# Read weights turned by VectorE blocks and on-chip transfers instead of TensorE, and one store per 128 state rows

## The chip, the core and the metric

The kernel runs on one core of a Trainium2 chip. The core has a matrix engine (PE in the profile, with PEld for its weight loads), three elementwise engines (DVE, the vector engine; ACT, the scalar engine; POOL), a sync engine SP, and 16 DMA engines. DMAs here are issued by the sequencers of SP and ACT; each sequencer issues in program order and stops at the first DMA whose wait isn't met. The metric is the device time of one execution in microseconds. Measured time before: 678.72 us, the median of three runs (678.38 to 679.03).

## What is computed

```python
# x: [8 batches, 8 heads, 512 tokens, 64], state: [8, 8, 32 states, 64]
scores  = scale * x @ state^T              # [B, H, 512, 32]
a       = softmax over the 32 states
xread   = a @ state                        # tokens read the states
scores2 = scale * state @ x^T              # [B, H, 32, 512]
a2      = softmax over the 512 tokens
sread   = a2 @ x                           # states read the tokens
rows    = concat(xread, sread) over tokens # 8 * (512 + 32) = 4352 rows of 8 * 64 = 512
out     = relu(rows @ w_in)**2 @ w_out     # w_in 512 x 2048, w_out 2048 x 512
```

All of it is float32. The two large products are computed as three passes over high and low parts of the operands (`hi*hi + lo*hi + hi*lo`).

## The kernel before

**Per batch, the tokens.** Head products are packed: a tile of 128 rows is 4 heads (`HG`) times 32 states (`N`), and there are two such groups (`NG`). `scores` (L198) multiplies the states with the transposed tokens `xt_raw` into the PSUM tile `pst`. From it the softmax over states is made with the states turned onto the free axis: VectorE's 32x32 block transpose `turn1` (L245) into the tile `q1`, maximum, subtraction, exponential, sum, division, and the block transpose back, `turn2` (L278), into the tile `at`; then `at` is split into the parts `a_hi` (ScalarE) and `a_lo` (GpSimd for batches 2 to 7). The state is multiplied into `w_in` beforehand (`z_piece`, L131: tiles `pz`, `z_hi`, `z_lo`), so that the up product of the MLP is `ph = z^T a` (L364), six matmuls of 512 columns per block of 128 hidden units. ScalarE applies the relu (`r`), VectorE squares in place, ScalarE rounds to `g_hi`, VectorE subtracts to `g_lo`, and twelve matmuls (L407) add the block into four PSUM tiles `po`. Such a step of 6 + 12 matmuls is repeated 16 times per batch, and the down product of a block is issued two blocks after its up product.

**Per batch, the states.** `keep` (L217) copies `pst` to the tile `e`, and `exps2` (L220) makes the exponentials of the softmax over tokens in it, with the row sums in `s2`. To multiply them with the tokens, the tokens have to lie on the partitions. `turn` (L308) does that with eight 128x128 TensorE transposes into the PSUM tile `pt` and one ScalarE copy to the tile `e_t` (L316). `read` (L318) then multiplies `e_t` with the tokens `xn_raw` in 32 small matmuls, one per group, head and block of 128 tokens (L325, tile `pr`), VectorE scales by the row sums (`rd`, L330), and GpSimd puts the result into the row tile `sr`. After the last batch the 256 state rows go through the same MLP in a stage of their own (`states`, L826), which ends the program: its two output tiles of 128 rows are copied from PSUM and stored (L858).

**What sets the order.** Batches 0 and 1 up to their last up product are ordered by an explicit list scheduler (`Plan`); everything after is emitted in slots, two per step of 18 matmuls. A queue of attention steps (`reads`) is worked off over the slots so that each batch's is done in time; the table `lags` says how many slots a step must lie behind another (L579 to L581). The states' read of batch b - 2 is queued ahead of the scores of batch b. A scheduler behind the source then moves instructions by a model of its own, and the order on each engine is fixed when the program is built. All these PSUM tiles (`pst`, later `pz`, `pt`, `pr`) share one buffer, tag `px`. The SBUF tile `e_t` shares its buffer with `at` (tag `at`, one buffer), so `e_t` of a batch can only be written when both parts have been made from the next batch's `at`.

Of the kernel before, what the change touches and what calls it, by code (L numbers as in the profile page):

```python
# [9 lines left out]
F32 = mybir.dt.float32  # L10
# [8 lines left out]
def memory_attention_then_relu2_ffn(  # L19
# [21 lines left out]
    nc = tc.nc  # L41
    P = 128
    B, S, C = xn.shape
    D = stP.shape[1] // 2
    H = C // D
    N = stP.shape[2] // (H // 2)
    DM, DF = w_out.shape[1] // 2, w_out.shape[0]
    R = S + N
    NG = H * N // P
    HG = H // NG  # L50
    NCC = DM // P
    NFC = DF // P
    NT = S // P
    ZC = 4
    GB = P // N
# [10 lines left out]
    sb = ctx.enter_context(tc.tile_pool(name="sb", bufs=2))  # L66
    ps_o = ctx.enter_context(tc.tile_pool(name="ps_o", bufs=4, space=bass.MemoryType.PSUM))
    ps_h = ctx.enter_context(tc.tile_pool(name="ps_h", bufs=2, space=bass.MemoryType.PSUM))
    ps_x = ctx.enter_context(tc.tile_pool(name="ps_x", bufs=1, space=bass.MemoryType.PSUM))
# [5 lines left out]
    ident = const.tile([P, P], F32, name="ident")  # L75
# [15 lines left out]
    def split(*args):  # L91
        for step in parts_of(*args):
            step()
# [76 lines left out]
    def attention(b):  # L170
        NJ = S // 32
        pair, my = [], {}
# [133 lines left out]
            return turn1, soft1, soft1b, soft1c  # L306

        def turn():  # L308
            pt = ps_x.tile([P, NG, NT, P], F32, name="pt", tag="px")
            for g in range(NG):  # L310
                for t in range(NT):
                    nc.tensor.transpose(  # L312
                        out=pt[:, g, t, :], in_=my["e2"][:, g, t * P:(t + 1) * P], identity=ident
                    )
            my["e"] = sb.tile([P, NG, NT, P], F32, name="e_t", tag="at", bufs=1)
            nc.scalar.copy(out=my["e"], in_=pt)  # L316

        def read():  # L318
            pr = ps_x.tile([P, NG, S], F32, name="pr", tag="px")
            with tc.high_priority(offset=HURRY):  # L320
                for g in range(NG):
                    for t in range(NT):
                        for j in range(HG):
                            h = g * HG + j
                            nc.tensor.matmul(  # L325
                                pr[j * N:(j + 1) * N, g, :D], lhsT=my["e"][:, g, t, j * N:(j + 1) * N],
                                rhs=my["n"][:, t, h * D:(h + 1) * D], start=t == 0, stop=t == NT - 1,
                            )
            rd = sb.tile([P, NG, D], F32, name="rd", bufs=1)
            nc.vector.tensor_mul(  # L330
                out=rd, in0=pr[:, :, :D], in1=my["s2"].rearrange("p (g o) -> p g o", o=1)
                .broadcast_to([P, NG, D])
            )
            at = (b % GB) * N
            for j in range(HG):
                nc.gpsimd.tensor_copy(  # L336
                    out=sr[b // GB][at:at + N, j * NG * D:(j + 1) * NG * D],
                    in_=rd[j * N:(j + 1) * N].rearrange("p g d -> p (g d)"),
                )

        steps = dict(
            pad=pad, load_t=load_t, scores=scores, keep=keep, exps2=exps2, load_n=load_n, turn=turn,
            read=read,
        )
        return pair, steps, [soft(gs) if b < 2 else grouped(*soft(gs)) for gs in halves]
# [87 lines left out]
    def move(t, dst, po):  # L433
        if t % 2:
            nc.scalar.copy(out=dst, in_=po)
        else:
            nc.vector.tensor_copy(out=dst, in_=po)
# [35 lines left out]
    begins, ends, at = {}, {}, {}  # L473
# [102 lines left out]
    lags = {}  # L576
    for b in range(B):
        _, w, softs = attentions[b]
        lags[w["exps2"]] = [(w["scores"], 1)]  # L579
        lags[w["turn"]] = [(w["exps2"], 1)]  # L580
        lags[w["read"]] = [(w["turn"], 1)]  # L581
        if b > 1:
            lags[softs[0][2]] = [(softs[0][1], 1)]

# [14 lines left out]
    for n, (b, fcs) in enumerate(parts):  # L599
        i = fcs[0]  # L600
# [225 lines left out]
    def states():  # L826
        NS = B * N
        x2 = []

        def turn2(i):  # L830
            def run():
                if not x2:
                    x2.extend(
                        sb.tile([P, NCC, NS], F32R, name=n, tag=t, bufs=2)
                        for n, t in (("x2_hi", "a_hi"), ("x2_lo", "a_lo"))
                    )
                own = slice(i * P, (i + 1) * P)
                pt = ps_x.tile([P, NCC, P], F32, name="pt2", tag="px")
                for cc in range(NCC):
                    nc.tensor.transpose(  # L840
                        out=pt[:, cc, :], in_=sr[i][:, cc * P:(cc + 1) * P], identity=ident
                    )
                split(x2[0][:, :, own], x2[1][:, :, own], pt, nc.vector)
            return run

        def first(fc):
            while reads.done < len(reads.steps):
                reads.next()
            w_hi = sb.tile([P, NCC, P], F32R, name="wi_hi", tag="z_hi", bufs=2)
            w_lo = sb.tile([P, NCC, P], F32R, name="wi_lo", tag="z_lo", bufs=2)  # L850
            split(w_hi, w_lo, wi[:, :, fc * P:(fc + 1) * P], nc.vector)
            return [
                (w[:, cc, :], v[:, cc, :])
                for w, v in ((w_hi, x2[0]), (w_lo, x2[0]), (w_hi, x2[1]))
                for cc in range(NCC)
            ]

        def rows(t, po):  # L858
            tile_ = sb.tile([P, DM], F32, name="os_", tag="raw", bufs=RAW)
            move(t, tile_, po)  # L860
            for i in range(GB):
                at = (t * GB + i) * R + S
                queue = nc.scalar if i % 2 else nc.sync
                queue.dma_start(out=out[at:at + N, :], in_=tile_[i * N:(i + 1) * N, :])

        reads.add([turn2(i) for i in range(NGB)], 2 * ends[B - 1] - 2, 2 * ends[B - 1] - 8)
        return dict(width=NS, fcs=range(NFC), first=first, rows=rows)

    mlp([batch(*p) for p in parts] + [states()], begin, aux)
# [34 lines left out]
```

## Time and profile before

| | |
|---|---|
| median of three runs | 678.72 us |
| the profiled execution | 678.34 us, of which 676.2 us lie between its first and last instruction (the span) |
| PE busy | 646.4 us, 96% of the span |
| DVE, ACT, POOL busy | 368.0, 288.9, 24.3 us |
| DMA | 43.59 MB in 15803 packets |
| TensorE transposes of the read weights | 64 |
| ScalarE copies of the transposed weights | 8 |
| stores of state rows | 8, of 64 KB each |

The page gives the busy time of each engine, its busy share in 40 slices of the span, the chain of work that ended last, and groups of instructions by source line. The trace behind it answers for single lines, for tiles (by name), and for stretches of time. In a timeline row the numbers are the start and the duration in us, then engine, line, operation, output and input tiles, shape and count; in brackets stands how long the engine had been idle and who ended that. Several equal instructions in a row are merged: the duration is then from the first start to the last end.

### The profile page before, as it was taken

To read this page: it belongs to the slowest core of one execution; us is meant where nothing else is said; L and a number is where in the kernel's file an instruction comes from. 1 tells how busy PE (TensorE), PEld (TensorE's weight loads), DVE (VectorE), ACT (ScalarE), POOL (GpSimd) and SP (SyncE) were. 2 spreads that over 40 slices of the span, in tenths; PEclk is the share of its full clock that TensorE was granted. 3 is DMA by queue.
4 is the path that set the end of the run, shared out by engine and by line. 5 is a ranking of instruction groups with operands and counts; after the bars stand their busy time and mean duration, and the time that the engine had idled before them with its cause. 6 is when DMAs were issued, how large, how long until landed. Compare 5 with 4: busy or idle time off the path is not lost.

```text
span 676.2 us, 9543 instructions
## 1 busy us (share of the span) xinstructions
PE 646.4 (96%) x3864; PEld 492.8 (73%) x3864; DVE 368.0 (54%) x522; ACT 288.9 (43%) x468; POOL 24.3 (4%) x44
## 2 busy tenths in 40 slices
PE   1788999999999999999999999999999999999996
PEld 0465876777777777777777877777778767888995
DVE  4899789346557336533483347433563254333553
ACT  3567665344435335333442335323353233333442
POOL 0000000000101000100010000100010000000000
PEclk9999999999999999999999999999999999999999
DMA  8534560013040005000310005000301001000101
GB/s 318 187 131 181 182 230 31 1 67 126 34 153 5 1 0 189 4 1 1 127 65 0 1 1 188 0 1 1 126 1 63 1 1 62 1 0 1 63 1 32
DMA packets 15803, 43.59 MB, mean 64 GB/s; under 512 B 1296, under 2 KB 3344, under 8 KB 13840
## 3 DMA queue, kind: packets, MB, share of 16 engines
q1 hardware_dynamic: 15568, 42.73, 17.3%
q8 instruction: 30, 0.49, 0.3%
q10 hardware_dynamic: 192, 0.26, 0.2%
q14 instruction: 13, 0.11, 0.1%
HBM read 34.08 MB, written 8.91 MB: 64 GB/s over the span
## 4 chain that ended last, share of the span: by engine, by line
PE 89%; DVE 7%; issue 1%; ACT 1%; DMA 1%; SPq 0%; DVEq 0%; ACTq 0%
PE po L407 53%; PE ph L364 28%; PE pz L154 4%; PE pr L325 1%; PE pst L204 1%; PE pt L312 1%; DVE wof L114 1%; DMA xt_raw<-xT 1%; DVE wo_lo L87 1%; DVE z_lo L87 1%; DVE wi L114 1%; DVE wi L120 1%; DVE wi L108 0%; DVE g_lo L87 0%; DVE a_lo L87 0%
## 5 line engine op out<-in xcount | busy, mean ns | idle before, releaser
L407 PE MATMUL po<-wo_hi,g_hi 128*128 128x512 f32 x544 | 215.4, 396 | 0.1
L407 PE MATMUL po<-wo_lo,g_hi 128*128 128x512 f32 x544 | 213.5, 392 | 0.8 <-DVE wo_lo L87 0.8
L369 ACT ACTIVATE r<-ph 128x512 f32<-128x512 f32 (+1 forms) x144 | 82.9, 576 | 174.4 <-PE ph L364 174.0
L407 PE MATMUL po<-wo_hi,g_lo 128*128 128x512 f32 x544 | 154.3, 394 | 0.0
L377 DVE TENSOR_TENSOR ph<-ph,r 128x512 f32<-128x512 f32 (+1 forms) x128 | 84.9, 663 | 126.0 <-ACT r L369 125.6
L87 DVE TENSOR_TENSOR g_lo<-ph,g_hi 128x512 fp32r<-128x512 f32 (+1 forms) x144 | 94.7, 658 | 73.9 <-ACT g_hi L84 44.5
L84 ACT CAST g_hi<-ph 128x512 fp32r<-128x512 f32 (+1 forms) x144 | 81.0, 563 | 110.3 <-DVE ph L377 79.3
L407 PEld LDWEIGHTS po<-wo_hi,g_hi 128*128 128x128 f32 x544 | 102.2, 188 | 29.6 <-ACT g_hi L84 4.4
L407 PEld LDWEIGHTS po<-wo_lo,g_hi 128*128 128x128 f32 x544 | 102.2, 188 | 27.9 <-issue 5.0
L407 PEld LDWEIGHTS po<-wo_hi,g_lo 128*128 128x128 f32 x544 | 100.3, 188 | 28.0 <-issue 7.1
L364 PE MATMUL ph<-a_hi,z_lo 128*128 128x512 f32 x256 | 82.8, 402 | 3.2 <-DVE z_lo L87 3.2
L364 PE MATMUL ph<-a_hi,z_hi 128*128 128x512 f32 x256 | 82.4, 403 | 3.0 <-ACT a_hi L84 2.0
L364 PE MATMUL ph<-a_lo,z_hi 128*128 128x512 f32 x256 | 80.2, 395 | 0.0
L87 DVE TENSOR_TENSOR z_lo<-pz,z_hi 128x1024 fp32r<-128x1024 f32 (+2 forms) x37 | 39.7, 1078 | 52.4 <-ACT z_hi L84 52.3
L364 PEld LDWEIGHTS ph<-a_hi,z_lo 128*128 128x128 f32 x256 | 47.9, 190 | 23.0 <-issue 8.4
L364 PEld LDWEIGHTS ph<-a_hi,z_hi 128*128 128x128 f32 x256 | 47.8, 190 | 18.3 <-ACT a_hi L84 2.7
L84 ACT CAST z_hi<-pz 128x1024 fp32r<-128x1024 f32 (+2 forms) x37 | 32.9, 899 | 55.9 <-PE ph L364 34.6
L364 PEld LDWEIGHTS ph<-a_lo,z_hi 128*128 128x128 f32 x256 | 48.7, 190 | 10.8
L154 PE MATMUL pz<-wi,sp_raw 64*32 64x512 f32 (+2 forms) x560 | 36.4, 579 | 10.7 <-DVE wi L120 8.6
L154 PEld LDWEIGHTS pz<-wi,sp_raw 64*32 64x32 f32 x560 | 6.5, 107 | 25.1 <-DVE wi L120 10.2
L336 POOL COPY sr<-rd 32x128 f32<-32x128 f32 x32 | 9.2, 289 | 384.5 <-DVE rd L330 383.4
L246 DVE STREAM_TRANSPOSE q<-pst 128x1024 f32<-128x1024 f32 (+1 forms) x9 | 10.1, 1126 | 19.7 <-ACT e L218 11.1
(61 smaller groups left out, 381.6 us busy)
## 6 DMA issues: line engine op xcount, KB each, us to landing
xt_raw<-xT SPq DMA_DIRECT2D x8, 1024.0 KB, 5.5
wo_raw<-w_out SPq DMA_DIRECT2D x8, 1024.0 KB, 5.7
xn_raw<-xn SPq DMA_DIRECT2D x8, 1024.0 KB, 5.5
out<-sum SPq DMA_DIRECT2D x32, 256.0 KB, 3.5
wi_raw<-w_in SPq DMA_DIRECT2D x7, 1024.0 KB, 4.8
wi_raw<-w_in SPq DMA_DIRECT2D x2, 512.0 KB, 7.1
sp_raw<-stP SPq DMA_DIRECT2D x8, 64.0 KB, 1.8
out<-os__5348 SPq DMA_DIRECT2D x2, 64.0 KB, 1.7
```

Of the source, the lines that this page charges most:

```text
L84: nc.scalar.copy(out=hi, in_=src)
L87: eng_lo.tensor_sub(out=lo, in0=src, in1=hi.bitcast(F32))
L114: nc.vector.scalar_tensor_tensor(out=bits, in0=high, scalar=-0x80000000, in1=bits, op0=ALU.bitwise_and, op1=ALU.bitwise_or,)
L120: mark[:] = [nc.vector.scalar_tensor_tensor(out=bits, in0=low, scalar=29, in1=bits, op0=ALU.logical_shift_right, op1=ALU.bitwise_or,)]
L154: nc.tensor.matmul(pz[g][j * N:(j + 1) * N], lhsT=state[b][rows, j, :], rhs=wi[rows, j, cols], start=True, stop=True,)
L204: nc.tensor.matmul(pst[j * N:(j + 1) * N, g, :], lhsT=state[b][rows, j, :], rhs=my["t"][rows, j, :], start=True, stop=True,)
L246: nc.vector.transpose(out=my["q1"][:, gs].rearrange("p g j n -> p (g j n)"), in_=my["pst"][:, gs].rearrange("p g s -> p (g s)"),)
L336: nc.gpsimd.tensor_copy(out=sr[b // GB][at:at + N, j * NG * D:(j + 1) * NG * D], in_=rd[j * N:(j + 1) * N].rearrange("p g d -> p (g d)"),)
L364: nc.tensor.matmul(ph, lhsT=w, rhs=v, start=m == 0, stop=m == len(todo) - 1)
L369: nc.scalar.activation(r, my[0], AF.Relu)
L377: nc.vector.tensor_mul(out=ph, in0=ph, in1=r)
L407: nc.tensor.matmul(po[t], lhsT=g, rhs=w, start=i == 0 and j == 0, stop=i == last and j == 2)
```

## The change

`turn` no longer uses TensorE, PSUM or ScalarE. VectorE transposes the whole of `e` in 32x32 blocks into a new tile `eq`, which shares the buffer of `q1` (tag `q1`, one buffer). A 32x32 block transpose leaves each block where it was, so sixteen SBUF-to-SBUF transfers per batch, all on SP's queue, move the blocks to their places: the transfer for head `j` and token block `i` takes 32 partitions of `eq` with 2 x 4 pieces of 32 numbers (128 bytes) each, to 32 partitions of `e_t`. `e_t` has the same contents, addressed with the head as a dimension. `read` must now lie at least four slots behind `turn`, not one. At the end of the program each 128-row tile of state rows is stored by one transfer with an output pattern of 4 x 32 x 512, one on SP's queue and one on ACT's, instead of four transfers of 32 x 512, two on each.

```diff
         def turn():
-            pt = ps_x.tile([P, NG, NT, P], F32, name="pt", tag="px")
-            for g in range(NG):
-                for t in range(NT):
-                    nc.tensor.transpose(
-                        out=pt[:, g, t, :], in_=my["e2"][:, g, t * P:(t + 1) * P], identity=ident
+            eq = sb.tile([P, NG, NT, P // N, N], F32, name="eq", tag="q1", bufs=1)
+            nc.vector.transpose(
+                out=eq.rearrange("p g t i n -> p (g t i n)"),
+                in_=my["e2"].rearrange("p g s -> p (g s)"),
+            )
+            my["e"] = sb.tile([P, NG, NT, HG, N], F32, name="e_t", tag="at", bufs=1)
+            for j in range(HG):
+                for i in range(P // N):
+                    nc.sync.dma_start(
+                        out=my["e"][i * N:(i + 1) * N, :, :, j, :],
+                        in_=eq[j * N:(j + 1) * N, :, :, i, :],
                     )
-            my["e"] = sb.tile([P, NG, NT, P], F32, name="e_t", tag="at", bufs=1)
-            nc.scalar.copy(out=my["e"], in_=pt)
...
-                                pr[j * N:(j + 1) * N, g, :D], lhsT=my["e"][:, g, t, j * N:(j + 1) * N],
+                                pr[j * N:(j + 1) * N, g, :D], lhsT=my["e"][:, g, t, j, :],
...
-        lags[w["read"]] = [(w["turn"], 1)]
+        lags[w["read"]] = [(w["turn"], 4)]
...
-            for i in range(GB):
-                at = (t * GB + i) * R + S
-                queue = nc.scalar if i % 2 else nc.sync
-                queue.dma_start(out=out[at:at + N, :], in_=tile_[i * N:(i + 1) * N, :])
+            queue = nc.scalar if t % 2 else nc.sync
+            queue.dma_start(
+                out=out.rearrange("(b r) e -> b r e", r=R)[t * GB:(t + 1) * GB, S:, :],
+                in_=tile_,
+            )
```

The built order shows what moved. First TensorE, before the change, at the first batch's read weights (`pt` the transposes, `ph` and `po` the up and down products):

```order
L407 MATMUL po_588<-wo_hi,g_lo 128x512
L407 MATMUL po_589<-wo_hi,g_lo 128x512
L312 MATMUL pt<-ident,e_105 128x128 x8
L407 MATMUL po_1186<-wo_hi,g_hi 128x512
...
L407 MATMUL po_1189<-wo_hi,g_lo 128x512
L325 MATMUL pr<-xn_raw,e_t 32x64 x32
```

And the same place in the changed kernel:

```order
L411 MATMUL po_588<-wo_hi,g_lo 128x512
L411 MATMUL po_589<-wo_hi,g_lo 128x512
L329 MATMUL pr<-xn_raw,e_t 32x64 x32
L411 MATMUL po_1155<-wo_hi,g_hi 128x512
```

The eight transposes are gone, and the read stands where they stood. In all, 64 transposes leave TensorE. The read of batch 1 is now in three pieces (2, 1 and 29 matmuls) and that of batch 6 in two (3 and 29); before, the transposes of these two batches were in two pieces each.

Second VectorE, in the changed kernel, from the last batch's softmax (`at<-q`) to the read of batch 6 (`rd`); the second `eq` is batch 7's:

```order
L279 STREAM_TRANSPOSE at<-q_3931 128x1024
L87 TENSOR_TENSOR g_lo<-ph,g_hi 128x512
L310 STREAM_TRANSPOSE eq<-e_3355 128x1024
L381 TENSOR_TENSOR ph<-ph,r 128x512
...
L87 TENSOR_TENSOR g_lo<-ph,g_hi 128x512
L310 STREAM_TRANSPOSE eq<-e_3936 128x1024
L381 TENSOR_TENSOR ph<-ph,r 128x512
L87 TENSOR_TENSOR g_lo<-ph,g_hi 128x512
L334 TENSOR_TENSOR rd<-pr,s_3356 128x128
```

Each batch's `eq` is a new instruction on VectorE; but for the first and the last batch it stands one instruction behind `at<-q` of the next batch.

Third SP's queue, in the changed kernel, its last rows (`xn_raw` the tokens of the next read, `out` the stores):

```order
L317 DMA e_t<-eq 32x8x32 x16
L196 DMA xn_raw<-xn 128x4x512
L317 DMA e_t<-eq 32x8x32 x16
L824 DMA out<-sum 128x512 x8
L866 DMA out<-os__5412 4x32x512
```

The sixteen transfers of a batch stand together; those of batch 7 stand behind the token load of the same batch, and the store of a state tile is one row of 4 x 32 x 512.

## The prediction

> **What bounds the kernel now.** I read the page's busy shares first, then its chain of waits, then stretches of the trace.
>
> ```profile
> span 676.2 us, 9543 instructions
> PE 646.4 (96%) x3864; PEld 492.8 (73%) x3864; DVE 368.0 (54%) x522; ACT 288.9 (43%) x468; POOL 24.3 (4%) x44
> PEclk9999999999999999999999999999999999999999
> PE 89%; DVE 7%; issue 1%; ACT 1%; DMA 1%; SPq 0%; DVEq 0%; ACTq 0%
> ```
>
> TensorE is busy 96% of the span, with the granted clock in its top tenth throughout, and 89% of the chain that ended last is its work. A mean can hide stages, so I look at the stretches in which the changed parts lie (columns: stretch, its length, then busy us and count of PE, PEld, DVE, ACT, POOL, then granted clock, DMA share, GB/s).
>
> ```profile
> 145.00:157.00 12.00, 12.00 (x122) 9.27 (x127) 5.89 (x10) 5.64 (x10) 1.15 (x4) 1.00 0.47 177
> ...
> 262.00:335.00 73.00, 73.00 (x431) 56.11 (x424) 35.85 (x50) 28.39 (x45) 3.56 (x5) 1.00 0.11 38
> ...
> 480.00:530.00 50.00, 50.00 (x366) 39.00 (x366) 25.88 (x38) 20.56 (x33) 5.51 (x12) 1.00 0.18 64
> ```
>
> From the first transposes (145 us) to the last read (527 us) TensorE has no gap, and VectorE is busy half of the time. There an instruction taken from TensorE shortens the program by its own time, and work put on VectorE, ScalarE or a DMA costs nothing unless TensorE comes to wait for it.
>
> **What is removed.** The transposes of one batch in the timeline:
>
> ```profile
> 144.16 1.08 PE L407 MATMUL po<-wo_hi,g_lo 128*128 128x512 f32 x4
> 145.08 1.04 PE L312 MATMUL pt<-ident,e 128*128 128x128 f32 x8
> 145.94 0.50 PE L407 MATMUL po<-wo_hi,g_hi 128*128 128x512 f32 x1
> 146.28 0.39 PE L407 MATMUL po<-wo_lo,g_hi 128*128 128x512 f32 x1
> 146.51 0.40 PE L407 MATMUL po<-wo_hi,g_hi 128*128 128x512 f32 x1
> ```
>
> Matmuls overlap, so I count from start to start. A 512-column matmul follows the next by 0.23 us (146.28 to 146.51). Four from 144.16 would put the next at 145.07. The second matmul behind the transposes starts at 146.28, and without them it would have started at 145.07 + 0.23 = 145.30: the block costs 0.98 us. Eight batches: **-7.84 us**. The splits give a little back: the reads come in three pieces more than before and the transposes' two extra pieces are gone. Of the 0.98 us, eight starts at 0.11 us (1.04 less the last one's 0.27, by seven) are 0.88, so entering and leaving a block costs 0.1 for a transpose; for the read I allow 0.2 a piece, since it changes the tile shape of the array as well. Three times 0.2 less two times 0.1: **+0.4 us**.
>
> The ScalarE copies go too: 8 of about 1 us, on an engine that is not the bound, so nothing.
>
> **VectorE's block transposes.** The same operation on the same shape stands in the trace:
>
> ```profile
> L279 DVE STREAM_TRANSPOSE at<-q 128x1024 f32<-128x1024 f32 x7 | 8.6, 1236 | 0.0
> 170.89 1.24 DVE L279 STREAM_TRANSPOSE at<-q 128x1024 f32<-128x1024 f32 x1
> 172.04 0.66 DVE L87 TENSOR_TENSOR g_lo<-ph,g_hi 128x512 fp32r<-128x512 f32 x1
> 174.01 0.70 DVE L377 TENSOR_TENSOR ph<-ph,r 128x512 f32<-128x512 f32 x1 [1.31 <-ACT r L369]
> ```
>
> It is 1.24 us per batch, and in the new order it stands just behind that `g_lo`, where VectorE sat idle for 1.31 us. That hole covers it: 0. Without it each batch would be 1.24 us later on VectorE, and TensorE uses a block's `g_lo` two blocks on, so still little.
>
> **The sixteen transfers.** No row shows an SBUF-to-SBUF transfer, nor a 128-byte packet, so the price p of one of the sixteen is bounded. These are the nearest rows: stores issued back to back on SP, and a 64 KB load of 128 packets of 512 bytes, alone (its issue at 353.19, and the two stretches in which its packets run).
>
> ```profile
> 145.43 1.81 SPq L820 DMA_DIRECT2D out<-sum  x4
> 353.19 0.34 SPq L178 DMA_DIRECT2D sp_raw<-stP  x1
> 353.00:354.00 1.00, 1.00 (x12) 0.85 (x5) 0.49 (x1) 0.00 (x0) 1.00 (x1) 1.00 0.06 16
> 354.00:355.00 1.00, 1.00 (x6) 0.79 (x6) 0.00 (x0) 0.59 (x1) 0.51 (x1) 1.00 0.23 66
> xn_raw<-xn SPq DMA_DIRECT2D x8, 1024.0 KB, 5.5
> sp_raw<-stP SPq DMA_DIRECT2D x8, 64.0 KB, 1.8
> ```
>
> From below, issuing costs SP 1.81 / 4 = 0.45 us each. For the packets, a share of 0.06 + 0.23 of 16 engines for 1 us is 4.6 us over 128 packets, 36 ns each; one new transfer has 32 x 8 = 256 packets, so 256 x 36 / 16 = 0.58 us if a quarter-size packet costs as much. From above, transfers that didn't overlap at all would take the whole landing, 1.8 us. I take **p = 0.5**, between the two that are priced like the work, and 1.8 us behind the last issue until it lands: 16 x 0.5 + 1.8 = 9.8 us per batch. In the built program each of the sixteen also waits for the transfer issued eight before it; 8 x 0.45 = 3.6 us of issuing is longer than a landing of 1.8, so this adds nothing, but in batch 7, where the eighth before is the token load (5.5 us): some 2.4 us more there.
>
> What covers 9.8 us? Each batch's transfers start when GpSimd has read the next batch's `at` (the shared buffer), or, for the last, when the read before has freed `e_t`.
>
> ```profile
> 112.62 1.09 PE L154 MATMUL pz<-wi,sp_raw 64*32 64x512 f32 x16
> 118.69 0.16 DVE L233 TENSOR_SCALAR s<-s 128x2 f32<-128x2 f32 x1
> 156.57 1.09 PE L204 MATMUL pst<-xt_raw,sp_raw 64*32 64x512 f32 x16
> 173.35 2.39 POOL L87 TENSOR_TENSOR a_lo<-at,a_hi 128x1024 fp32r<-128x1024 f32 x1 [19.62 <-issue]
> ```
>
> The scores end at 157.6 and `a_lo` at 175.74, 18.1 us later. In the new order I count the matmuls from the scores to the read at 0.23 us, and 1.23 for each of the blocks of `pz` (its 1.09 with the way in and out). Batch 1: 108 matmuls and two blocks are 27.0 us to the first piece, 14.9 us behind `a_lo` for the piece that needs the last transfers. Batch 6: 123 and two blocks, and 8 more to the second piece: 14.4 us. Batch 7: its read lies 64 matmuls and a block, 15.8 us, behind the read of batch 6, with the 0.4 us issue of the token load ahead of it on SP (need 0.4 + 9.8 + 2.4 = 12.6). Batches 2 to 5 have 241 to 267 matmuls and four blocks, some 60 us less 18: over 40 us. Batch 0's `eq` follows the row at 118.69 us, and its read takes the place at 145 us: over 20 us. So all are covered: 0, with 3 to 5 us to spare in three batches.
>
> On SP nothing urgent is behind the transfers: the token loads there wait for the read before anyway.
>
> **The last stores.** They are on the path: nothing runs behind them.
>
> ```profile
> 671.27 0.81 SPq L864 DMA_DIRECT2D out<-os__5348  x2
> 671.27 0.88 ACTq L864 DMA_DIRECT2D out<-os__5348  x2
> 672.17 0.85 SPq L864 DMA_DIRECT2D out<-os__5354  x2
> 672.25 0.85 ACTq L864 DMA_DIRECT2D out<-os__5354  x2
> 671.00:672.00 1.00, 0.00 (x0) 0.00 (x0) 0.24 (x1) 0.37 (x1) 0.00 (x0) 1.00 0.00 0
> 672.00:673.00 1.00, 0.00 (x0) 0.00 (x0) 0.00 (x0) 0.00 (x0) 0.00 (x0) 1.00 0.85 223
> 673.00:674.00 1.00, 0.00 (x0) 0.00 (x0) 0.00 (x0) 0.00 (x0) 0.00 (x0) 1.00 0.92 246
> 674.00:675.00 1.00, 0.00 (x0) 0.00 (x0) 0.00 (x0) 0.00 (x0) 0.00 (x0) 0.94 0.17 55
> 561.00:565.00 4.00, 4.00 (x19) 3.27 (x18) 3.05 (x5) 2.35 (x5) 0.00 (x0) 1.00 0.65 247
> DMA packets 15803, 43.59 MB, mean 64 GB/s; under 512 B 1296, under 2 KB 3344, under 8 KB 13840
> ```
>
> Before, 256 rows of 2 KB keep all engines busy for 0.85 + 0.92 + 0.17 = 1.94 us, from 672.0 to about 674.2; that is 121 ns a row. In the stretch from 561 us four stores of 128 such rows take 0.65 x 4 x 16 / 512 = 81 ns a row. With one issue per queue the work could end about 0.4 us sooner: the lower bound, **-0.4**. The upper one comes from how a transfer is spread. The program issues 81 transfers, and 1296 packets under 512 bytes are 81 x 16: I read these as one completion per engine, so every transfer used 16 engines. Every one had an outermost dimension of 128 or 32. The new pattern's outermost dimension is 4. If the split goes along it, each store has four parts, both stores on the same four engines, and each engine moves 64 rows: 64 x 81 = 5.2 us, or 64 x 121 = 7.7, against 1.94. The end moves from 674.2 to between 677.2 and 679.7. I take the split into four, the one thing in which the new pattern differs, and 81 ns, since four engines crowd the memory less than sixteen: **+3.2 us**, bounds -0.4 and +5.5.
>
> The Trainium skill speaks against this store too ("DMA: Bandwidth & Descriptors", section "Why a DMA increments its semaphore by 16 and not by 1"): the largest engine count up to 16 that divides the slowest dimension of both patterns, and on these queues the lowest-numbered engines. By that rule it is 4 here, both stores on the same ones; the 1296 packets agree with it for the old patterns, and no row here shows a pattern of 4.
>
> **The sum.** -7.84 + 0.4 + 3.2 = -4.2 us. The profiled execution took 678.34 us (its span and 2.1 us around it), 0.38 below the median; 678.72 - 4.2 = **674.5 us**. About 0.2%, 1.4 us, is what a measurement of this kernel can tell from no change.
>
> **The rivals.**
>
> *The store is spread over 16 engines.* Then the last term is -0.4: 678.72 - 7.84 + 0.4 - 0.4 = 670.9. For it: all transfers so far were. Against it: none had so few outer rows. Chance 0.23.
>
> *The transfers come late at the three tight reads* (slower). TensorE then stands at the reads of batches 1, 6 and 7, and VectorE too: batch 7's `eq` waits in the shared buffer for batch 6's transfers, with squares and `g_lo` queued behind it. The three gaps sum to 45.1 us and the need is 48 p + 5.8, so it costs from p = 0.79, and eats the 4.2 us from p = 0.91. At p = 1.0 it is 2.9 + 3.4 + 2.4 = 8.7 us: 683.2. For it: the largest bound, 1.8, by which it would be 722. Against it: the stores above are issued at 0.45, and 0.58 already prices small packets as 512-byte ones. Chance 0.20.
>
> A rule for this rival is in the same page's "Specifications": below 512 bytes a transfer is read, modified and written. Were a packet's 36 ns doubled by it, p would be 1.15 and the time 690.4 by the same sum. The page also says, under "Why small descriptors are slow (HBM only)", that SBUF-to-SBUF traffic is spared; no row here shows either.
>
> **How the numbers follow.** The forecast has 0.57; its own range is 673 (no cost for the splits, 3.0 and a little less for the store) to 677 (5.5 for it). The range must hold 8 in 10: it takes in the 16-engine case at its low end, 670, and the forecast's upper part with a small delay at a read, 678.5; most of the late-transfer case stays out. Faster: 0.57 less 0.05 for the forecast's tail above 677.3, plus 0.23, plus 0.03 for a lateness that eats only part of the gain: 0.78. Same: that 0.05 and another 0.03 of the late case: 0.08. Slower: the rest of the late case, 0.14.
>
> **What would show it.** Right: 64 transposes fewer and no gap on TensorE from 145 to 520 us; in the steady batches the distance from one batch's scores to the next 1.0 us shorter; the `e_t` transfers landed within 10 us of their first issue and several us ahead of the read; a tail in which the DMA share stays near a quarter for over 5 us, and state stores that land more than 5 us behind their issue. Wrong: idle time of TensorE at `pr` ended by a DMA, idle time of VectorE at `eq` ended by a DMA, more than 0.8 us a transfer; or state stores that land in some 2 us.

## The result: 0.56% slower, where 0.6% faster was forecast

The changed kernel takes 682.35 us (median of four runs, 681.23 to 682.72) against 678.55 us before; the ratio is 1.0056, with a 95% interval of 1.0038 to 1.0075. The forecast was 674.5 us with a range of 670.0 to 678.5. It lies 7.8 us off, on the wrong side of no change.

The head of the page of the changed kernel, its chain of waits, and its DMA packets:

```profile
span 680.9 us, 9629 instructions
PE 646.5 (95%) x3800; PEld 487.7 (72%) x3800; DVE 376.7 (55%) x530; ACT 281.1 (41%) x460; POOL 24.2 (4%) x44
PE 90%; DVE 6%; issue 1%; ACT 1%; DMA 1%; SPq 0%; DVEq 0%; ACTq 0%
DMA packets 50501, 47.81 MB, mean 70 GB/s; under 512 B 35992, under 2 KB 38040, under 8 KB 48536
```

TensorE has 64 instructions fewer and is as busy as before: 646.5 us against 646.4. So something took its time back. The span is 4.7 us longer. Its end falls into two parts, the work up to the last output tile and the tail from the last stores on. The first row is of the kernel before, the others are of the changed kernel (timelines; the stores before stand in the prediction):

```profile
670.55 0.69 DVE L437 COPY os__5348<-po 128x512 f32<-128x512 f32 x1 [1.20 <-PE po L407]
670.15 0.69 DVE L441 COPY os__5412<-po 128x512 f32<-128x512 f32 x1 [1.20 <-PE po L411]
670.87 0.69 SPq L866 DMA_DIRECT2D out<-os__5412  x1
671.00 1.36 ACTq L866 DMA_DIRECT2D out<-os__5415  x1
```

The last output tile begins to leave PSUM at 670.15 us; before, that was at 670.55. All the work up to there gained 0.4 us, where 7.4 were forecast. From SP's store to the end of the span it takes 10.0 us (670.87 to 680.9), where it took 4.9 (671.27 to 676.2): the tail lost 5.1 us, where 3.2 were forecast.

**The tail.** Stretches of the changed kernel from the stores on (the column before the last is the DMA share):

```profile
671.00:673.00 2.00, 0.00 (x0) 0.00 (x0) 0.00 (x0) 0.00 (x0) 0.00 (x0) 1.00 0.12 13
673.00:675.00 2.00, 0.00 (x0) 0.00 (x0) 0.00 (x0) 0.00 (x0) 0.00 (x0) 0.53 0.22 50
675.00:677.00 2.00, 0.00 (x0) 0.00 (x0) 0.00 (x0) 0.00 (x0) 0.00 (x0) 0.50 0.26 102
677.00:679.00 2.00, 0.00 (x0) 0.00 (x0) 0.00 (x0) 0.00 (x0) 0.00 (x0) 0.50 0.24 92
```

The share stands at a quarter: four of sixteen engines. The packet counts say the same: 128 transfers of 256 small pieces are 32768, and 73 old and 128 new transfers with 16 completions each are 3216; that leaves 8 of the 35992 packets below 512 bytes, four for each of the two stores. ACT's queue, which carries one store and nothing else, has 132 packets on the page: 128 rows and 4 completions (before: 192, with 4 x 16). The sum of the shares is 0.84 x 2 = 1.68 us of all engines, 26.9 us of one engine, over 256 rows 105 ns a row (121 before); but now four engines carry them. The price is not even: in the first four microseconds shown only 126 KB move, 177 ns of an engine for a row; from 675 us on a row takes 84 ns (0.26 x 16 engines x 2 us over 100 rows).

**TensorE.** The lost time stands in one place, in batch 7. One `pz` block is torn (timeline of the changed kernel, from 495.8 us):

```profile
495.76 0.62 PE L368 MATMUL ph<-a_lo,z_hi 128*128 128x512 f32 x2
496.31 1.06 PE L154 MATMUL pz<-wi,sp_raw 64*32 64x512 f32 x6
497.30 0.49 PE L411 MATMUL po<-wo_lo,g_hi 128*128 128x512 f32 x1
497.72 1.04 PE L154 MATMUL pz<-wi,sp_raw 64*32 64x512 f32 x2
498.70 0.50 PE L411 MATMUL po<-wo_hi,g_hi 128*128 128x512 f32 x1
...
503.32 1.04 PE L154 MATMUL pz<-wi,sp_raw 64*32 64x512 f32 x2
504.30 0.74 PE L411 MATMUL po<-wo_hi,g_lo 128*128 128x512 f32 x2
```

(The trace counts two passes for one of these float32 matmuls: x6 is three, x2 is one.) A whole block of eight takes 1.09 us, and its tiles of 64 x 32 fill eight different parts of the array; I read this as running side by side. A lone one takes 1.04 us, and from one `po` to the next with a lone `pz` between them it is 1.40 us (497.30 to 498.70) where it would be 0.23. Five pieces too many are 5 x 1.17 = 5.9 us. The Trainium skill ("TensorEngine Tiling (Array Packing)", section "Key Properties") states that small tiles of the array work in parallel, and that a change of the tiling mode drains the engine first. The trace agrees with the first: eight together cost what one costs alone. How much of the 1.17 us is the drain, no run separates. No idle time appears; the profile counts the lone matmuls as busy (the groups of the kernel before, then of the changed one):

```profile
L154 PE MATMUL pz<-wi,sp_raw 64*32 64x512 f32 x480 | 32.7, 601 | 2.1 <-DVE z_lo L87 2.1
L325 PE MATMUL pr<-xn_raw,e_t 128*32 128x64 f32 x512 | 8.8, 221 | 0.0
L154 PE MATMUL pz<-wi,sp_raw 64*32 64x512 f32 x480 | 37.9, 601 | 1.7 <-DVE z_lo L87 1.7
L329 PE MATMUL pr<-xn_raw,e_t 128*32 128x64 f32 x512 | 9.7, 221 | 0.0
```

The `pz` matmuls went from 32.7 to 37.9 us, the reads from 8.8 to 9.7. The tear is in the built order of the changed kernel (a piece of 3, then five of 1, with a `po` matmul between each two); in the order of the kernel before, all blocks stand whole. The change did not touch `z_piece`. It moved the read and put the transfers into the stream that the scheduler works through.

**The transfers.** SP's queue in the changed kernel, first issue and time to the last, for four of the batches, and what they took of the engines in the middle of one:

```profile
120.48 10.54 SPq L317 DMA_DIRECT2D e_t<-eq  x16
170.41 10.78 SPq L317 DMA_DIRECT2D e_t<-eq  x16
498.81 10.39 SPq L317 DMA_DIRECT2D e_t<-eq  x16
520.72 0.40 SPq L196 DMA_DIRECT2D xn_raw<-xn  x1
521.42 11.35 SPq L317 DMA_DIRECT2D e_t<-eq  x16
e_t<-eq SPq DMA_DIRECT2D x128, 32.0 KB, 1.9
171.00:181.00 10.00, 10.00 (x47) 7.90 (x47) 4.56 (x7) 3.87 (x6) 0.00 (x0) 1.00 0.28 47
```

Sixteen issues take 10.5 us, 0.66 us each, and one lands 1.9 us after its issue. Batch 6's land at 511.1 us, batch 7's at 534.7; their reads begin at 517.3 and 536.7. TensorE's own list of waits has no DMA at a read; two of its rows:

```profile
PE pst L204 <- DMA xt_raw<-xT: 6.8, 1, 6.8
PE ph L368 <- DVE z_lo L87: 3.4, 2, 2.3
```

The first of them is the load at the program's start (6.5 us in the kernel before), and it is the only DMA in the list.

### The profile page after: what moved, and what is told of

Its sections match the earlier page's. It is cut to its first block, busy times and chain, and to the rows that moved or that the text cites. A ratio compares the mean times of both kernels' runs of the same rounds, so it can differ in the third digit from the quotient of the medians.

```text
span 680.9 us, 9629 instructions
## 1 busy us (share of the span) xinstructions
PE 646.5 (95%) x3800; PEld 487.7 (72%) x3800; DVE 376.7 (55%) x530; ACT 281.1 (41%) x460; POOL 24.2 (4%) x44
## 2 busy tenths in 40 slices
DMA packets 50501, 47.81 MB, mean 70 GB/s; under 512 B 35992, under 2 KB 38040, under 8 KB 48536
## 4 chain that ended last, share of the span: by engine, by line
PE 90%; DVE 6%; issue 1%; ACT 1%; DMA 1%; SPq 0%; DVEq 0%; ACTq 0%
PE po L411 53%; PE ph L368 28%; PE pz L154 5%; PE pst L204 1%; PE pr L329 1%; DMA xt_raw<-xT 1%; DVE wof L114 1%; DVE wo_lo L87 1%; DVE z_lo L87 1%; DVE wi L114 1%; DVE wi L120 1%; DVE a_lo L87 0%; DVE q L276 0%; DVE m L252 0%; ACT wof L105 0%
## 5 line engine op out<-in xcount | busy, mean ns | idle before, releaser
L154 PE MATMUL pz<-wi,sp_raw 64*32 64x512 f32 (+2 forms) x560 | 41.6, 579 | 10.3 <-DVE wi L120 8.6
```

The lines of the kernel that those rows point to most:

```text
L154: nc.tensor.matmul(pz[g][j * N:(j + 1) * N], lhsT=state[b][rows, j, :], rhs=wi[rows, j, cols], start=True, stop=True,)
```

## Experiments

The theory after the result: the torn `pz` block cost 5.9 us, the store over four engines 5.1 us, and the transposes were worth what they were priced at. The rival that the prediction named, transfers that come late, was still to be tested where the torn block no longer gives them time.

### Each cause undone alone, and both

The first repair changes one number in `z_due`, the function that emits the z pieces in the slot stage: how many instructions ahead of its place a piece is scheduled (`HURRY` is 120).

```diff
-            with tc.high_priority(offset=HURRY):
+            with tc.high_priority(offset=150):
                 for step in z_piece(b, cover, False):
```

In the built order this joins the torn block and moves nothing else on any engine:

```
-L154 MATMUL pz<-wi,sp_raw 32x512 x3
+L154 MATMUL pz<-wi,sp_raw 32x512 x8
 L411 MATMUL po_3823<-wo_lo,g_hi 128x512
-L154 MATMUL pz<-wi,sp_raw 32x512
 L411 MATMUL po_3824<-wo_hi,g_hi 128x512
-L154 MATMUL pz<-wi,sp_raw 32x512
```

On the kernel before, the same number changes nothing in the order of any engine.

> The changed kernel with the z pieces of the slot stage scheduled 150 instead of 120 instructions ahead; in the built order this only joins the one torn pz block of the last batch (pieces of 3, 1, 1, 1, 1, 1 matmuls between po matmuls) into one piece of 8, on TensorE, and nothing else moves. Theory (the torn block took back what the transposes gave): in the trace of the changed kernel each lone pz matmul costs about 1.4 us from the po before it to the second po behind it instead of 0.23, so five extra pieces are 5 x 1.17 = 5.9 us; expected 682.4 - 5.9 = 676.5 us, TensorE ahead of the changed kernel by 5.9 us from the block on. Rival (the sixteen transfers of batches 6 and 7 come late): the transfers of batch 6 land at 511.1 us and the read would now come at 511.4, those of batch 7 need 14.3 us behind the read of batch 6; if they set the pace the gain is mostly lost in waits at pr: 680 or more, with idle time of TensorE ended by a DMA.

Measured: 676.41 us, 0.9975 of the kernel before (0.9966 to 0.9984). The gain is 5.9 us, as worked out from the trace. The block and the reads in its timeline and groups, with the transfers of batches 6 and 7 on SP:

```profile
496.66 1.09 PE L154 MATMUL pz<-wi,sp_raw 64*32 64x512 f32 x16
511.86 0.31 PE L329 MATMUL pr<-xn_raw,e_t 128*32 128x64 f32 x6
514.14 1.08 PE L329 MATMUL pr<-xn_raw,e_t 128*32 128x64 f32 x58
531.26 1.10 PE L329 MATMUL pr<-xn_raw,e_t 128*32 128x64 f32 x64
L154 PE MATMUL pz<-wi,sp_raw 64*32 64x512 f32 x480 | 32.7, 601 | 1.7 <-DVE z_lo L87 1.7
499.20 10.39 SPq L317 DMA_DIRECT2D e_t<-eq  x16
515.95 10.91 SPq L317 DMA_DIRECT2D e_t<-eq  x16
```

The time of `pz` is back at 32.7 us. The last transfer of batch 6 lands at 511.5 us (499.20 + 10.39 + 1.9). The first piece of its read, from 511.86, takes three heads and needs only the first twelve transfers; the fourth head, which needs the last four, comes with the second piece at 514.14. For batch 7, whose read is whole, the last one lands at 528.8 and the read begins at 531.26. The rival does not come true: the transfers are covered by 2.6 and 2.5 us.

The second repair puts the old store back: the two lines with one transfer per tile are replaced by the loop over four (the diff of the change, its last part, reversed).

> The changed kernel with the state rows stored as before, four transfers of 32 x 512 per tile on both queues. Theory (the 4 x 32 x 512 store runs on four engines): the tail from the end of the last PSUM copy shrinks from 10.0 us to the 5.0 us of the kernel before, 682.4 - 5.1 = 677.3 us, DMA share of the tail back to 0.85 to 0.92 for 2 us. Rival (the tail is long for another reason, such as the program's end at a halved clock): no change, 682.

Measured: 677.13 us, 5.2 less than the changed kernel, 0.9983 of the kernel before (0.9974 to 0.9992). In its tail the stores run on all engines again:

```profile
671.00:672.00 1.00, 0.00 (x0) 0.00 (x0) 0.00 (x0) 0.00 (x0) 0.00 (x0) 1.00 0.27 66
672.00:673.00 1.00, 0.00 (x0) 0.00 (x0) 0.00 (x0) 0.00 (x0) 0.00 (x0) 1.00 1.00 264
673.00:674.00 1.00, 0.00 (x0) 0.00 (x0) 0.00 (x0) 0.00 (x0) 0.00 (x0) 0.59 0.67 195
```

> Both repairs together. If the two causes are independent: 682.4 - 5.9 - 5.1 = 671.4 us, below the kernel before by 7.2 us, which is what the 64 transposes were priced at (7.84) less the torn reads. If the transfers come late at the last two reads: 675 or more. If either cause is wrong, its part of the gain is missing.

Measured: 671.15 us, 0.9894 of the kernel before (0.9879 to 0.9910). The two repairs add up: 5.9 and 5.2 alone, 11.2 together. What is left is the change of the transpose by itself, a gain of 7.2 us.

### The new store on the kernel before

> The kernel before with the state rows stored by one 4 x 32 x 512 transfer per tile, nothing else. Theory (four engines): 678.6 + 5.1 = 683.7 us, DMA share of the tail near 0.25 for 7 us. Rival (the long tail belongs to the transfers of the read weights or their semaphores): 678.6, unchanged.

Measured: 683.38 us against 678.37, ratio 1.0077 (1.0065 to 1.0090): 5.0 us, with nothing else changed. Its tail shows the same quarter:

```profile
673.00:675.00 2.00, 0.00 (x0) 0.00 (x0) 0.00 (x0) 0.00 (x0) 0.00 (x0) 1.00 0.23 46
675.00:677.00 2.00, 0.00 (x0) 0.00 (x0) 0.00 (x0) 0.00 (x0) 0.00 (x0) 0.66 0.26 101
```

These rows also speak against a halved clock as the cause, the rival named for the old store: from 673 to 675 us the granted clock is 1.00 here and 0.53 in the changed kernel, and the engines move 46 and 50 GB/s.

### The store with an outermost dimension of two

On the kernel with whole z pieces:

```diff
             queue = nc.scalar if t % 2 else nc.sync
-            queue.dma_start(
-                out=out.rearrange("(b r) e -> b r e", r=R)[t * GB:(t + 1) * GB, S:, :],
-                in_=tile_,
-            )
+            for i in range(0, GB, 2):
+                queue.dma_start(
+                    out=out.rearrange("(b r) e -> b r e", r=R)[t * GB + i:t * GB + i + 2, S:, :],
+                    in_=tile_[i * N:(i + 2) * N, :],
+                )
```

> Whole z pieces, and each state tile stored by two transfers of 2 x 32 x 512 instead of one of 4 x 32 x 512. Theory (a transfer is split over as many engines as its outermost dimension, always the same first ones): all four transfers on two engines, 128 rows each instead of 64; the stores run for some 14 us at a DMA share near 0.125 instead of 7 us near 0.25, so 676.4 + 7 = 683.4 us. Rival (the store is slow because one transfer is one long chain, or each transfer gets its own engines): with two transfers per queue the tail is the same or shorter, 674 to 676.

Measured: 682.30 us, 5.9 more than with one transfer of four (7 were expected; 64 more rows for an engine at the 84 ns of the later rows are 5.4). The tail, in stretches of 2 us:

```profile
667.00:669.00 2.00, 0.00 (x0) 0.00 (x0) 0.00 (x0) 0.00 (x0) 0.00 (x0) 0.63 0.12 33
669.00:671.00 2.00, 0.00 (x0) 0.00 (x0) 0.00 (x0) 0.00 (x0) 0.00 (x0) 0.50 0.13 33
...
675.00:677.00 2.00, 0.00 (x0) 0.00 (x0) 0.00 (x0) 0.00 (x0) 0.00 (x0) 0.50 0.13 50
677.00:679.00 2.00, 0.00 (x0) 0.00 (x0) 0.00 (x0) 0.00 (x0) 0.00 (x0) 0.50 0.08 32
```

The share is an eighth, two engines, although four transfers are under way on two queues. Outermost dimensions of 32, 4 and 2 give 16, 4 and 2 engines, and several transfers share the same ones: here the rule cited in the prediction from "DMA: Bandwidth & Descriptors" of the Trainium skill is borne out. Which engines they are by number, no run here shows. Here too the first rows are the dear ones: 0.12 and 33 GB/s are 119 ns a row, 0.13 and 50 GB/s are 85.

### More torn blocks in the kernel before

The same number as in the first repair, on the kernel before, set to 80. In the built order the `pz` blocks then stand in 21 more pieces.

> The kernel before with the z pieces of the slot stage scheduled only 80 instructions ahead: in the built order pz blocks stand in 21 more pieces than before, nearly all of them lone matmuls between po or ph matmuls; some other matmuls change place. Theory (a torn pz piece costs about 1.17 us wherever it stands): 678.4 + 21 x 1.17 = 703 us. Rival (the six pieces of the changed kernel were dear because of what stood beside them in the last batch, such as the transfers): less than half of that, under 690.

Measured: 702.99 us, ratio 1.0365 (1.0345 to 1.0385): 24.5 us for 21 pieces, 1.17 us each. The group and two of the lone matmuls:

```profile
L154 PE MATMUL pz<-wi,sp_raw 64*32 64x512 f32 x480 | 54.4, 601 | 2.0 <-DVE z_lo L87 2.0
221.87 1.04 PE L154 MATMUL pz<-wi,sp_raw 64*32 64x512 f32 x2
223.26 1.04 PE L154 MATMUL pz<-wi,sp_raw 64*32 64x512 f32 x2
```

On average, the price of a piece does not depend on this change or on the last batch. It also shows what the number does: at 120 the kernel before has no torn block, at 80 it has many. That the sixteen added transfers use up the head start of 120 because it is counted in instructions is how I explain the tear; no run tested it.

### The transfers in another order, and twice as many

With both repairs, the loops over `j` and `i` in `turn` exchanged, so that all heads become complete together:

```diff
-            for j in range(HG):
-                for i in range(P // N):
+            for i in range(P // N):
+                for j in range(HG):
                     nc.sync.dma_start(
```

> Whole z pieces and the old store, and the sixteen transfers in another order (token block outermost, head inside). The heads' parts of e_t then become complete together at the end, and in the built order the reads of batches 1 and 6 are in two pieces each of 3 and 29 (before: 2, 1, 29 and 3, 29), with one scores block that tears a ph pair no longer. Theory (each further piece of a block of small matmuls costs TensorE some tenths of a microsecond, 1.0 for the scores between two ph matmuls at most): 0.3 to 1 us less than the kernel with both repairs, 670.3 to 670.9. Rival (the transfers' landing sets the pace of the reads of batches 1 and 6, so that their pieces cost nothing): 671.2 or more.

Measured: 671.02 us, 0.9894 of the kernel before (0.9880 to 0.9909). It is the fastest of all by its median, but 0.13 us less than the other order is no difference that these runs can tell. The expected 0.3 to 1.0 did not show; the reads are busy for 9.4 us instead of 9.7, too little to be seen in the time.

With both repairs, each transfer cut in two by group:

```diff
-                        out=my["e"][i * N:(i + 1) * N, :, :, j, :],
-                        in_=eq[j * N:(j + 1) * N, :, :, i, :],
+                        out=my["e"][i * N:(i + 1) * N, 0, :, j, :],
+                        in_=eq[j * N:(j + 1) * N, 0, :, i, :],
+                    )
+                    nc.sync.dma_start(
+                        out=my["e"][i * N:(i + 1) * N, 1, :, j, :],
+                        in_=eq[j * N:(j + 1) * N, 1, :, i, :],
                     )
```

> Whole z pieces and the old store, with each of the sixteen transfers cut in two by group: 32 per batch, each of 32 x 4 pieces of 128 bytes instead of 32 x 8. The scheduler moves the reads of batches 1, 6 and 7 later to suit. Theory A (the price of a transfer is SP's issue, 0.66 us whatever the number of pieces): 32 x 0.66 = 21 us from the first to the last issue of a batch, and if the reads still come behind, the time stays within 1.5 us of 671.2; if they don't, TensorE waits at pr for a DMA and the time rises by several us. Theory B (the price goes with the pieces): 32 x 0.33 = 10.6 us as with sixteen, no wait, 670 to 673.

Measured: 678.96 us, 7.8 more than with sixteen. From its timelines and groups, and the wait instructions within one whole read (the last row):

```profile
120.44 0.60 SPq L317 DMA_DIRECT2D e_t<-eq  x1
121.08 0.60 SPq L321 DMA_DIRECT2D e_t<-eq  x1
L333 PE MATMUL pr<-xn_raw,e_t 128*32 128x64 f32 x512 | 15.7, 222 | 0.1
328.33 1.71 PE L333 MATMUL pr<-xn_raw,e_t 128*32 128x64 f32 x64
L333 PEldq EVENT_SEMAPHORE  x8: 51/51/51, 328.5 to 329.3; - x8
```

A transfer with half the pieces still takes 0.64 us from issue to issue: the price is SP's, per transfer, not per piece (theory A). The time was lost in another way than expected. TensorE shows no wait for a DMA; the reads themselves are busy for 15.7 us, 6.0 more than with sixteen. A read that stands in one piece takes 1.71 us instead of 1.10, and in the built order those of batches 1, 6 and 7 are torn into eleven pieces, with sixteen transfers into six. One thing in the trace fits the 0.6 us of a whole read: eight wait instructions of 51 ns, 0.41 us together, now stand between its matmuls (328.5 to 329.3 us). With sixteen transfers the same read has all its eight before its first matmul (322.0 to 324.2, read from 326.24). No run tested this, and the 1.8 us beyond the reads were not taken apart.

## Why the prediction was wrong

**The bound.** Right: TensorE sets the pace from 145 us on. SP's token loads, which follow the reads, show a batch's period, first in the kernel before, then in the changed one:

```profile
330.45 0.38 SPq L196 DMA_DIRECT2D xn_raw<-xn  x1
404.68 0.38 SPq L196 DMA_DIRECT2D xn_raw<-xn  x1
328.10 0.39 SPq L196 DMA_DIRECT2D xn_raw<-xn  x1
401.43 0.39 SPq L196 DMA_DIRECT2D xn_raw<-xn  x1
```

The period went from 74.23 to 73.33 us. That is 0.90 us a batch, where 1.0 was predicted for this view and 0.98 in the sum.

**The term that was missing.** "-7.84" for eight blocks and "+0.4" for splits gave -7.4; with both repairs it is -7.2, with an interval from 6.1 to 8.2. So these terms were right together; neither is shown by itself, and the 0.2 for a piece of the read was an allowance that no run isolates. But the sum left out the torn `pz` block, 5.9 us. It stood in the built order, which showed whether blocks were whole. The prediction looked there for the pieces of the read and priced three of them, but counted the `pz` matmuls of the same stretch as whole blocks ("Batch 6: 123 and two blocks", one of which is the torn one). This is the step that failed: the sum put the order of the matmuls that the change does not touch at nothing, without a reason, and the runs showed 5.9 us there.

**The store.** The mechanism was right, four engines for both stores; the size was not, and this term is the second thing that failed. "+3.2" was worked out at 81 ns a row, the lower of two prices (its own end times, 674.2 and 677.2, give 3.0), and measured were 5.0 to 5.3 us, near the upper bound of 5.5. A row cost 105 ns on average. For the later rows 81 was nearly right, 84 ns; missing was the slow start, in which the first 62 rows or so cost 177 ns each. What makes the first rows dear, no run shows. The rival with sixteen engines is refuted.

Put together: 674.5 + 5.9 + 1.9 = 682.3 us, and 682.35 were measured.

**The transfers.** p was taken as 0.5 and is 0.66; sixteen land within 12.4 us, not 10. They were hidden all the same, as forecast, since p stayed under the 0.79 from which waits were worked out. Once the block is whole, 2.6 and 2.5 us are left at the reads of batches 6 and 7, where 4.6 and 3.2 were worked out. The bound from the packets, 36 ns each, was far too high: a share of 0.28 for 10 us is 44.8 us of engine time for some 15 transfers of 272 packets, 11 ns each. What binds is SP's issue, as the run with 32 transfers shows, and it is dearer for this pattern than the 0.45 us of a plain store. So the rival of late transfers did not decide. The prediction's estimate after the Trainium skill ("DMA: Bandwidth & Descriptors", "Specifications"), 36 ns doubled because transfers below 512 bytes are read, modified and written, was further off still; whether the 11 ns hold such a step, no run shows.

**VectorE.** Right: it has 8.7 us more work (376.7 against 368.0) and no matmul waits for it; one weight load of a read waits 0.4 us for an `eq`.

## What to carry to other kernels

Before pricing a change in a kernel whose order a scheduler makes, compare the built orders over the whole program and count the pieces of every block of small packed matmuls, those the change does not touch too: a lone one costs as much as the whole block. A transfer at the end of a program should keep a large outermost dimension; merging stores to save issues can cost engines. Once both were mended, turning the weights off TensorE gave 1.06%.

## What was not expected of the hardware

- A packed block of eight float32 matmuls (64 x 32 tiles, 512 columns) takes 1.09 us and one alone 1.04 us; each further piece costs 1.17 us, the same for 5 pieces in one kernel and 21 in another.
- SP needs 0.60 to 0.66 us to issue one of the strided on-chip transfers, whether of 256 or 128 pieces, where it needs 0.34 for a plain load of 128 rows.
- A 128-byte piece between SBUF and SBUF occupies an engine for about 11 ns, so 512 KB in 4096 such pieces load the sixteen engines to 28% only, while they are issued.
- A 2 KB row of the last stores costs an engine 121 ns when sixteen engines work, and 84 ns late in the store when four or two do; the first rows of the store over four cost 177 ns.
- Tearing and store are invisible in the busy shares: TensorE is busy 95% with 5.9 us of its time lost inside busy blocks.
